# Attention followed by an MoE layer on one core: joined score and value groups on TensorE, and a written order for all engines

## The chip, the core and the metric

The kernel runs on one core of a Trainium2 chip. The metric is the device time of one execution in microseconds. Lower is better. Before the change three runs took 991.96, 991.89 and 991.86 us; the median is 991.89.

The engines in the text: TensorE (PE; its weight loads are PEld), VectorE (DVE), ScalarE (ACT), GpSimd (POOL) and SyncE (SP), which issues most DMAs. Matmul results land in PSUM banks of 512 float32 columns; eight banks exist. All other tiles lie in SBUF.

## The reference

```python
B, H, Sl, Sg, D = 8, 8, 512, 32, 64; window = 32
s_g   = scale * q_g @ [k_g, k_l].T                    # global queries see all keys
out_g = softmax(s_g) @ [v_g, v_l]
s_l   = [scale * q_l @ k_g.T, where(|i - j| <= window, scale * q_l @ k_l.T, -1e9)]
out_l = softmax(s_l) @ [v_g, v_l]                     # local queries: globals and a band
x     = concat([out_g, out_l], tokens) as (B * 544, 512)
h     = x @ w_in                                      # 512 -> 2048
out   = softplus(h) @ w_out                           # 2048 -> 512
```

## The kernel before

A **pair** m is two heads of one batch; there are 32 pairs, four to a batch (m = 4b + j). Pairs 0 to 3 (batch 0) go through an attention of their own at the start (`scores0` to `split0g`). The others run while the second layer already works on an earlier batch.

**The second layer.** A **block** b is one batch: 512 local tokens, 16 **tiles** f of 128 hidden columns. For a tile, `hpart` makes h in one PSUM bank with twelve matmuls of 512 columns (four slices j of x; each the high half xh against both halves of the weights, and the low half xl against one). `act` then makes e: three rows on ScalarE (abs, exp, ln), one on VectorE (line 533, the last reader of the bank of h), gh on ScalarE and gl on GpSimd. `opart` multiplies gh and gl by the output weights into four output banks o0 to o3, six matmuls for two of them. The output half of a tile comes one or two tiles behind its h (`moe_items`). Block 8 is the global tokens of all batches. `split_x` makes xh and xl of the next block from the attention's result xa; slices with odd j on VectorE, the others on ScalarE and GpSimd.

**Attention of a pair.** `scores` makes the scores of 512 queries for two heads in two pieces, p = 0 and 1, with matmuls that use half of TensorE's rows (64x128); each piece fills the two banks of the pool `ps_a`. VectorE adds the mask (line 312) and so copies the piece to SBUF as s; then it takes maxima of 32x32 blocks into mt (313). `maxima` gathers them: GpSimd copies three quarters next to the first (325), VectorE reduces (328 to 332) and copies the result to three more quarters (338). `probs` spreads the maxima as mb (346), GpSimd subtracts (355, 357) and ScalarE takes the exponential (358). `sums` does the same for the sums: zt (368), the gathering, a small addition (371), reciprocals zr (375) and rb (377). `values` makes v_ps with matmuls of half of TensorE's columns (128x64) in the banks of `ps_a`; VectorE multiplies them with rb into xa (396).

**PSUM.** `ps_h` has two banks, which only h uses; `ps_a` has two, for s_ps and v_ps in turn; four are for the output.

**Order.** Behind the start only TensorE's order is written out in full (`mm`); on the other engines the scheduler chooses between what is ready by its own estimate. The attention's steps are a list with a position each (`pieces`): scores of pair m at 12m and 12m + 6, sums at 12m + 14, values at 12m + 21; they are let in between the second layer's items as these advance (48 positions a block). So four pairs pass in a block, each with three separate visits of TensorE: piece 0, piece 1 and the values. Pair 8 begins in block 0.

Of the kernel before, what the change touches and what calls it, by code (L numbers as in the profile page):

```python
# [19 lines left out]
P = 128  # L20
# [3 lines left out]
NPC = 2  # L24
# [9 lines left out]
MPE = 8  # L34
LAG_Z = 6
# [28 lines left out]
def moe_over_global_local_attention(  # L64
# [31 lines left out]
    mask0 = pl.tile([P, 2, 2, 224], BF16, tag="rb", name="mask0", bufs=1)  # L96
# [38 lines left out]
    M = B * H // 2  # L135
    st = {}
# [179 lines left out]

    def grid(t, start, *dims):
        base = t[0:32, start:start + 1]
        return bass.AP(base.tensor, base.offset, [list(base.ap[0])] + [list(d) for d in dims])

    def gather(mt, op):
        for a in range(1, 4):
            nc.gpsimd.tensor_copy(mt[0:32, GW * a:GW * a + GW], mt[32 * a:32 * a + 32, 0:GW])  # L325
        e0 = 4 * GW + 1
        for u, off in ((-1, 2), (2, 3)):
            nc.vector.tensor_reduce(grid(mt, e0 + u, (7, 6), (1, 2)), grid(mt, 4 + u - 2 * (u < 0), (12, 6), (1, 2), (off, 2), (GW, 4)), axis=AX.XY, op=op)
        nc.vector.tensor_reduce(grid(mt, e0 + 1, (7, 6), (4, 2)), grid(mt, 4 + 1, (12, 6), (7, 2), (GW, 4)), axis=AX.X, op=op)
        g = e0 + 42  # L330
        nc.vector.tensor_reduce(grid(mt, g, (1, 2)), grid(mt, 4 + 4, (36, 2), (12, 3), (3, 2), (GW, 4)), axis=AX.XYZ, op=op)
        nc.vector.tensor_copy(grid(mt, e0 + 4, (21, 2), (7, 3)), mt[0:32, g:g + 2].unsqueeze(2).to_broadcast([32, 2, 3]))  # L332
        return mt[:, e0:e0 + 42]

    def maxima(m):
        e = gather(st.pop(("mt", m)), ALU.max)
        for a in range(1, 4):
            i = nc.vector.tensor_copy(e[32 * a:32 * a + 32, 0:40], e[0:32, 0:40]).ins
        order["maxima"] = i
        st["e", m] = e  # L340

    def probs(m, p):
        s, e = st["s", m, p], st["e", m]
        k = QW[p] // 32
        mb = pl.tile([P, 2, 352], F32, tag="mb", name=f"mb{m}_{p}", bufs=2)
        nc.vector.transpose(mb[:, :, :QW[p]].rearrange("p h (s k) -> p h s k", k=32),  # L346
                            windows(e, FIRST[p], 21, 2, k).unsqueeze(3).to_broadcast([P, 2, k, 32]))

        def pairs(t, width, start, step, w):
            base = t[:, 0, start:start + 1]  # L350
            return bass.AP(base.tensor, base.offset, [list(base.ap[0]), [width, 2], [step, 2], [1, w]])

        for so, sd, mo, md, w in (((0, 352, 0, 192, 160),), ((32, 192, 0, 128, 192),))[p]:
            sw = pairs(s, 512, so, sd, w)
            nc.gpsimd.tensor_tensor(sw, sw, pairs(mb, 352, mo, md, w), op=ALU.subtract)  # L355
        for so, mo, w in (((160, 64, 192),), ((0, 64, 32), (416, 224, 96)))[p]:
            nc.gpsimd.tensor_tensor(s[:, :, so:so + w], s[:, :, so:so + w], mb[:, :, mo:mo + w], op=ALU.subtract)  # L357
        nc.scalar.activation(s, s, AF.Exp, scale=0.125)  # L358
# [4 lines left out]

    def sums(m):
        zt = pl.tile([P, rows_of(349)], F32, tag="mt", name=f"zt{m}", bufs=3)
        nc.gpsimd.memset(windows(zt, 0, 36, 3, 4), 0.0)
        for p in range(NPC):
            nc.vector.tensor_reduce(windows(zt, 4 + 16 * p, 36, 2, 16), st["s", m, p].rearrange("p h (b k) -> p h b k", k=32),  # L368
                                    axis=AX.X, op=ALU.add, apply_transpose=True)
        z = gather(zt, ALU.add)  # L370
        nc.vector.tensor_scalar(z[0:32, 0:40], z[0:32, 0:40], 1e-9, None, op0=ALU.add)
        zr = pl.tile([P, ROW], F32, tag="zr", name=f"zr{m}", bufs=2)
        for a in range(4):
            h = a // 2
            nc.vector.reciprocal(zr[32 * a:32 * a + 32, 0:19], z[0:32, 21 * h:21 * h + 19])
        rb = st["rb", m] = pl.tile([P, rows_of(608)], F32, tag="rb", name=f"rb{m}", bufs=1)[:, 0:608]
        nc.vector.transpose(rb.rearrange("p (s k) -> p s k", k=32), zr[:, 0:19].unsqueeze(2).to_broadcast([P, 19, 32]))

    def values(m):
        b, j = divmod(m, H // 2)  # L380
        vt = st.pop(("v", m))
        ps = ps_a.tile([P, 2, 512], F32, tag="a", name=f"v_ps{m}")
        parts = ((0, 0, 0, 160, 0, 0), (1, 0, 160, 192, 0, 64), (2, 0, 352, 160, 0, 192), (2, 1, 0, 32, 0, 352), (3, 1, 32, 96, 0, 288),
                 (3, 1, 128, 96, 1, 0), (4, 1, 224, 192, 1, 32), (5, 1, 416, 96, 1, 128))
        seen = set()
        for c, p, o, w, bank, at in parts:
            for h in range(2):
                mm(ps[64 * h:64 * h + 64, bank, at:at + w], lhsT=vt[:, h, c], rhs=st["s", m, p][:, h, o:o + w],
                   start=(bank, h) not in seen, stop=(c, bank) in ((3, 0), (5, 1)), skip_group_check=True)
                seen.add((bank, h))  # L390
        for p in range(NPC):
            del st["s", m, p]
        rb = st.pop(("rb", m))
        y = xa[b, j] = pl.tile([P, 608], F32, tag="xa", name=f"xa{b}_{j}", bufs=4)
        for bank, at, w in ((0, 0, 384), (1, 384, 224)):
            nc.vector.tensor_tensor(y[:, at:at + w], ps[:, bank, 0:w], rb[:, at:at + w], op=ALU.mult)  # L396
        for o in (352, 576):
            nc.gpsimd.tensor_tensor(y[:, 128:160], y[:, 128:160], y[:, o:o + SG], op=ALU.add)
        nc.sync.dma_start(out=xg_dram[j, :, SG * b:SG * b + SG], in_=y[:, 128:160])
        ready.add((b, j))  # L400

# [3 lines left out]
    def pieces():  # L405
        def piece(*fs):
            def go():
                for f in fs:
                    f()
            return go  # L410
        ps = []
        for m in range(M0, M):
            for p in range(NPC):
                fs = [lambda m=m, p=p: scores(m, p)]
                if m + 1 < M:
                    fs.append(lambda m=m, p=p: load(m + 1, p))
# [4 lines left out]
            ps.append((12 * m + 8 + LAG_Z, lambda m=m: sums(m)))  # L421
            fs = [lambda m=m: values(m)]
            if m + 2 < M:
                fs.append(lambda m=m: load_v(m + 2))
            ps.append((end(m), piece(*fs)))
        ps.sort(key=lambda t: t[0])
        return ps


    def split_x(b, j):  # L430
        xh[j] = pl.tile([P, 512], F32R, tag=f"xh{j}", name=f"xh{b}_{j}", bufs=1)
# [70 lines left out]
    def moe_items():  # L502
# [24 lines left out]
        def act(b, f):  # L527
            ph = g.pop(("ps", b, f))
            e = pl.tile([P, 512], F32, tag="e", name=f"e{b}_{f}", bufs=2)
            nc.scalar.activation(e, ph, AF.Abs)  # L530
            nc.scalar.activation(e, e, AF.Exp, scale=-1.0)  # L531
            nc.scalar.activation(e, e, AF.Ln, bias=one)  # L532
            nc.vector.scalar_tensor_tensor(e, ph, 0.0, e, op0=ALU.max, op1=ALU.add)  # L533
            gh = pl.tile([P, 512], F32R, tag="gh", name=f"gh{b}_{f}", bufs=3)
            gl = pl.tile([P, 512], F32R, tag="gl", name=f"gl{b}_{f}", bufs=3)
            nc.scalar.copy(gh, e)  # L536
            nc.gpsimd.tensor_tensor(gl, e, gh.bitcast(F32), op=ALU.subtract)  # L537
# [14 lines left out]
        def store(b, t):  # L552
            o = pl.tile([P, 512], F32, tag=("gh", "gl")[t % 2], name=f"ot{b}_{t}", bufs=3)
            if b < B:
                if t % 2:
                    nc.scalar.copy(o, po[t])
                else:
                    nc.vector.tensor_copy(o, po[t])
                r = b * S + SG + t * P
                nc.sync.dma_start(out=out[r:r + P, :], in_=o)  # L560
            else:
                nc.scalar.copy(o[:, 0:256], po[t][:, 0:256])
                nc.vector.tensor_copy(o[:, 256:512], po[t][:, 256:512])
# [11 lines left out]
        done = 0  # L575
        for i, (b, f) in enumerate(tiles):
            if f == 0 and b > 0:
                items.append((b, 0, 0, lambda b=b: [split_x(b, j) for j in range(4)]))
# [5 lines left out]
            behind = 1 if (b, f + 1) not in tiles or (f == 0 and b > 0) else 2  # L584
            upto = halves.index(tiles[i - behind] + (0,)) + (2 if tiles[i - behind][0] < B else 1) if i >= behind else 0
            while done < upto:
                second(done, b)
                done += 1
        while done < len(halves):
# [87 lines left out]
    for i, (b, size, w, it) in enumerate(items):  # L677
        it()
# [5 lines left out]
        at = first + 48 * (b + gone[b] / total[b]) if b else START + (first + 48 - START) * gone[b] / total[b]  # L684
        attention(at)
# [59 lines left out]
```

## Time and profile before

| | |
|---|---|
| profiled execution | 991.48 us, of which the span is 989.7 |
| median of three runs | 991.89 us |
| granted TensorE clock, mean | 0.988 |
| TensorE, output matmuls of gh (L132, 1,088) | 344.8 us |
| TensorE, h matmuls of xh (L132, 1,152) | 341.9 us |
| ScalarE rows of e and gh (L530, 531, 532, 536), 136 each | 81.0, 85.9, 98.4, 84.5 us |
| VectorE row of e (L533), 136 | 92.7 us |
| GpSimd row of gl (L537), 136 | 180.5 us |

A row names the line, the engine, the operation and the tiles, then count, busy time and the mean of one. "Idle before" an engine's row is put down to whatever released it last. A chain row gives start, length, engine, tile and line, and how many records it merges; a full matmul is one record, and each float32 matmul of the attention is two. Matmuls of a row overlap, so a group's length is read from start to start.

### The profile page before, as it was taken

What the parts mean: (1) busy time and instruction counts of PE and PEld (TensorE: products, weight loads), DVE (VectorE), ACT (ScalarE), POOL (GpSimd) and SP (SyncE); (2) the same over time, 40 slices, a digit from 0 to 9 for tenths busy, and PEclk for the clock granted to TensorE, in tenths of its full rate; (3) what the DMA queues carried; (4) which work ended last, traced back from release to release, by engine and by line L of the source; (5) the groups of instructions that cost most, each with busy time, mean ns of one, the idle gap of its engine ahead of it and who ended that gap; (6) DMA issues with size and microseconds to landing.
All of it is one profiled execution on the core that took longest, in us unless ns stands there. A gap on an engine that the chain in (4) does not pass through costs nothing.

```text
span 989.7 us, 14732 instructions
## 1 busy us (share of the span) xinstructions
PE 946.2 (96%) x5476; PEld 763.8 (77%) x5476; DVE 643.1 (65%) x1193; ACT 492.6 (50%) x811; POOL 469.5 (47%) x648
## 2 busy tenths in 40 slices
PE   6998598889999999999999999999999999999998
PEld 4776476668888788878887888878887888888896
DVE  5869898896667756786669666776668665411211
ACT  5756466544444544454445444454454445444453
POOL 4437776655445544444445544554445444322221
PEclk8998899999999999999999999999999999999999
DMA  9651331211112211121112111121112100100000
GB/s 357 231 188 46 122 111 57 65 66 41 47 47 69 69 47 46 48 74 47 47 37 72 47 47 47 66 71 47 47 33 88 32 17 1 65 1 1 10 35 22
DMA packets 30697, 64.60 MB, mean 65 GB/s; under 512 B 7328, under 2 KB 7840, under 8 KB 30624
## 3 DMA queue, kind: packets, MB, share of 16 engines
q1 hardware_dynamic: 29888, 63.32, 19.0%
q8 instruction: 43, 0.70, 0.3%
q10 hardware_dynamic: 736, 0.33, 0.2%
q14 instruction: 30, 0.25, 0.1%
HBM read 54.20 MB, written 9.44 MB: 64 GB/s over the span
## 4 chain that ended last, share of the span: by engine, by line
PE 67%; DVE 9%; POOL 4%; issue 3%; ACT 1%; DMA 1%; POOLq 0%; DVEq 0%; ACTq 0%
PE o L132 30%; PE h L132 29%; PE s_ps L132 5%; PE v_ps L132 4%; DVE xh L442 1%; DVE zt L368 1%; DVE xl L443 1%; POOL xl L443 1%; DVE mb L346 1%; POOL mt L325 1%; DVE s L312 1%; POOL s L355 1%; DVE xa L396 1%; DVE mt L332 0%; DVE e L533 0%
## 5 line engine op out<-in xcount | busy, mean ns | idle before, releaser
L132 PE MATMUL h<-xh,wi 128*128 128x512 f32 (+1 forms) x1152 | 341.9, 380 | 6.5 <-DVE e L533 5.8
L132 PE MATMUL o<-wo,gh 128*128 128x512 f32 x1088 | 344.8, 398 | 0.0
L537 POOL TENSOR_TENSOR gl<-e,gh 128x512 fp32r<-128x512 f32 x136 | 180.5, 1327 | 315.7 <-ACT gh L536 263.2
L132 PEld LDWEIGHTS h<-xh,wi 128*128 128x128 f32 x1152 | 211.1, 188 | 51.8 <-DVE e L533 8.9
L132 PEld LDWEIGHTS o<-wo,gh 128*128 128x128 f32 x1088 | 198.8, 188 | 46.0 <-issue 3.3
L533 DVE SCALAR_TENSOR_TENSOR e<-h,e 128x512 f32<-128x512 f32 x136 | 92.7, 682 | 210.1 <-ACT e L532 192.5
L132 PE MATMUL h<-xl,wi 128*128 128x512 f32 (+1 forms) x576 | 217.6, 378 | 0.9 <-DVE xl L443 0.9
L132 PE MATMUL o<-wo,gl 128*128 128x512 f32 x544 | 213.1, 392 | 0.2
L530 ACT ACTIVATE e<-h 128x512 f32<-128x512 f32 x136 | 81.0, 595 | 175.5 <-PE h L132 173.5
L536 ACT CAST gh<-e 128x512 fp32r<-128x512 f32 x136 | 84.5, 622 | 154.7 <-DVE e L533 154.5
L132 PEld LDWEIGHTS h<-xl,wi 128*128 128x128 f32 x576 | 108.4, 188 | 21.7 <-DVE xl L443 1.3
L355 POOL TENSOR_TENSOR s<-s,mb 128x640 f32<-128x640 f32 (+1 forms) x56 | 96.6, 1725 | 57.8 <-DVE mb L346 57.8
L132 PEld LDWEIGHTS o<-wo,gl 128*128 128x128 f32 x544 | 102.4, 188 | 23.2 <-POOL gl L537 1.1
L368 DVE TRANSPOSE_TENSOR_REDUCE zt<-s 128x32 f32<-128x1024 f32 x56 | 69.4, 1239 | 58.9 <-ACT s L358 58.7
L358 ACT ACTIVATE s<-s 128x1024 f32<-128x1024 f32 x56 | 59.4, 1061 | 83.5 <-POOL s L357 47.7
L532 ACT ACTIVATE e<-e,one 128x512 f32<-128x512 f32 x136 | 98.4, 723 | 4.3
L531 ACT ACTIVATE e<-e 128x512 f32<-128x512 f32 x136 | 85.9, 632 | 3.9
L313 DVE TRANSPOSE_TENSOR_REDUCE mt<-s 128x32 f32<-128x1024 f32 x56 | 68.9, 1231 | 3.7 <-ACT s L310 2.9
L132 PE MATMUL s_ps<-raw 64*128 64x192 f32 (+2 forms) x672 | 64.3, 325 | 0.6 <-issue 0.6
L132 PEld LDWEIGHTS v_ps<-s,v 128*64 128x64 f32 x896 | 49.4, 137 | 19.5 <-ACT s L310 6.5
L132 PE MATMUL v_ps<-s,v 128*64 128x96 f32 (+3 forms) x896 | 56.7, 280 | 7.3 <-ACT s L310 5.2
L132 PEld LDWEIGHTS s_ps<-raw 64*128 64x128 f32 x672 | 53.5, 192 | 11.6 <-issue 10.8
(147 smaller groups left out, 886.0 us busy)
## 6 DMA issues: line engine op xcount, KB each, us to landing
raw<-in_qk SPq DMA_DIRECT2D x32, 352.0 KB, 3.0
v<-in_v SPq DMA_DIRECT2D x28, 384.0 KB, 3.0
raw<-in_qk SPq DMA_DIRECT2D x28, 368.0 KB, 3.6
wiraw<-in_w_in SPq DMA_DIRECT2D x16, 512.0 KB, 8.5
woraw<-in_w_out SPq DMA_DIRECT2D x16, 512.0 KB, 7.4
out<-ot SPq DMA_DIRECT2D x32, 256.0 KB, 2.1
v<-in_v SPq DMA_DIRECT2D x4, 512.0 KB, 8.6
raw<-in_qk SPq DMA_DIRECT2D x4, 416.0 KB, 8.3
```

What stands on the lines that cost most here:

```text
L132: order["pe"] = after(nc.tensor.matmul(*a, **k), "pe").ins
L313: order["scores"] = nc.vector.tensor_reduce(windows(mt, 4 + 16 * p, 36, 2, 16), s.rearrange("p h (b k) -> p h b k", k=32), axis=AX.X, op=A ...
L355: nc.gpsimd.tensor_tensor(sw, sw, pairs(mb, 352, mo, md, w), op=ALU.subtract)
L358: nc.scalar.activation(s, s, AF.Exp, scale=0.125)
L368: nc.vector.tensor_reduce(windows(zt, 4 + 16 * p, 36, 2, 16), st["s", m, p].rearrange("p h (b k) -> p h b k", k=32), axis=AX.X, op=ALU.add ...
L443: (nc.vector if j % 2 else nc.gpsimd).tensor_tensor(lo, f(t), hi.bitcast(F32), op=ALU.subtract)
L530: nc.scalar.activation(e, ph, AF.Abs)
L531: nc.scalar.activation(e, e, AF.Exp, scale=-1.0)
L532: nc.scalar.activation(e, e, AF.Ln, bias=one)
L533: nc.vector.scalar_tensor_tensor(e, ph, 0.0, e, op0=ALU.max, op1=ALU.add)
L536: nc.scalar.copy(gh, e)
L537: nc.gpsimd.tensor_tensor(gl, e, gh.bitcast(F32), op=ALU.subtract)
```

## The change

**Joined scores.** For pairs 8 to 31 `scores_all` makes both pieces in one stretch of matmuls. Piece 0 goes to the two banks of `ps_a`, piece 1 to the two banks of `ps_h`, one for each head. The mask of piece 0 is added by one VectorE row, that of piece 1 by two.

**Joined values.** `values_two` makes the values of an odd pair in `ps_a` and of the even pair before it in the two banks of `ps_h`, in one stretch.

**Places.** `later` names the tile of a block at which each step is written: scores at tiles 2, 4, 9 and 11, values of two pairs at 8 and 15, and the other steps in between. Around a group, output halves are put off so that six output matmuls stand right behind it. Pair 8 no longer begins in block 0. At tile 15 the next block's first two slices of x are split ahead of the values.

**Order.** In blocks 1 to 6 every instruction of VectorE, ScalarE and GpSimd runs in the order in which it is written (`inorder`); semaphores still decide when.

**Small rows.** The copies of lines 332 and 338 become `tensor_reduce` over an axis of one. In blocks 2 to 7 the xh casts are all on ScalarE, and xl of slices 2 and 3 is on VectorE. rb has two buffers.

```diff
+MLAST = 7
+S_AT = (2, 4, 9, 11)
+V_AT = (8, 15)
+PRE = (3, 3)
+    def inorder(i):
+        if strict:
+            k = "in " + str(i.ins.engine)
+            order[k] = after(i, k).ins
+        return i
+    def scores_all(m):
+        ps = ps_a.tile([P, 2, 512], F32, tag="a", name=f"s_ps{m}_0")
+        banks2 = [[ps[:, h] for h in range(2)], [ps_h.tile([P, 512], F32, tag="h", name=f"s_ps{m}_1{h}") for h in range(2)]]
+        for p in range(NPC):
+            for c, qs, o, w in PARTS[p]:
...
+        inorder(nc.vector.tensor_tensor(st["s", m, 0], ps, mask[:, 0].unsqueeze(1).to_broadcast([P, 2, 512]), op=ALU.add))
+        for h in range(2):
+            inorder(nc.vector.tensor_tensor(st["s", m, 1][:, h], banks2[1][h], mask[:, 1], op=ALU.add))
...
-            i = nc.vector.tensor_copy(e[32 * a:32 * a + 32, 0:40], e[0:32, 0:40]).ins
+            i = inorder(nc.vector.tensor_reduce(e[32 * a:32 * a + 32, 0:40], e[0:32, 0:40].unsqueeze(2), axis=AX.X, op=ALU.max)).ins
...
+    def values_two(m):
+        values(m + 1, a_banks(m + 1))
+        values(m, [ps_h.tile([P, 512], F32, tag="h", name=f"v_ps{m}_{i}") for i in range(2)])
+        values_out(m)
+        values_out(m + 1)
+    def later():
+        for m in range(MLAST + 1, M):
+            b, i = divmod(m - 4, H // 2)
+            at = NF * b + S_AT[i]
+            put(at, "group", lambda m=m: scores_all(m), lambda m=m: spread(st["mt", m]))
...
+            put(at + 1, "act", lambda m=m: maxima(m, True), *[lambda m=m, p=p: lift(m, p) for p in range(NPC)], lambda m=m: probs(m, 0, False))
+            put(at + 2, "act", lambda m=m: exps(m, 0), lambda m=m: probs(m, 1, False))
+            put(at + 3, "act", lambda m=m: exps(m, 1))
+            if m % 2:
+                at = NF * b + V_AT[i // 2]
+                put(at - 1, "end", lambda m=m: sums_first(m))
+                if i // 2:
+                    put(at, "act", lambda b=b: split_x(b + 1, 0), lambda b=b: split_x(b + 1, 1))
+                put(at, "act", lambda m=m: sums_rest(m))
+                put(at, "group", lambda m=m: values_two(m - 1))
+            else:
+                put(at + 4, "act", lambda m=m: sums_first(m))
+                put(at + 5, "act", lambda m=m: sums_rest(m))
...
-            (nc.vector.tensor_copy if j % 2 else nc.scalar.copy)(hi, f(t))
-            (nc.vector if j % 2 else nc.gpsimd).tensor_tensor(lo, f(t), hi.bitcast(F32), op=ALU.subtract)
+            onv = j >= 2 if 1 < b < B else j % 2
+            inorder((nc.vector.tensor_copy if onv and not 1 < b < B else nc.scalar.copy)(hi, f(t)))
+            inorder((nc.vector if onv else nc.gpsimd).tensor_tensor(lo, f(t), hi.bitcast(F32), op=ALU.subtract))
```

Three places show what moves. The first is on TensorE in block 2, at the second piece of a pair's scores (s_ps_1 is piece 1 before; s_ps_0 is piece 0, and s_ps_10 and s_ps_11 are the two heads of piece 1 in the change). Before:

```order
L132 MATMUL o_1_3031<-wo_825,gh_4_3156 128x512 x2
L132 MATMUL o_1_3031<-wo_825,gl_4_3157 128x512
L132 MATMUL s_ps_1_3268<-raw_1_3047,raw_0_2927 128x32 x2
L132 MATMUL s_ps_1_3268<-raw_1_3047 128x192 x4
L132 MATMUL s_ps_1_3268<-raw_1_3047 128x96 x2
L132 MATMUL o_2_3071<-wo_825,gh_4_3156 128x512 x2
L132 MATMUL o_2_3071<-wo_825,gl_4_3157 128x512
```

And in the change:

```order
L136 MATMUL s_ps_0_3094<-raw_0_3004 128x192 x2
L136 MATMUL s_ps_0_3094<-raw_0_3004 128x160 x2
L136 MATMUL s_ps_10_3095<-raw_1_3006,raw_0_3004 128x32
L136 MATMUL s_ps_11_3096<-raw_1_3006,raw_0_3004 128x32
L136 MATMUL s_ps_10_3095<-raw_1_3006 128x192
L136 MATMUL s_ps_11_3096<-raw_1_3006 128x192
```

The piece stood alone between output matmuls; now it follows piece 0 with nothing in between.

The second place is TensorE behind h of tile 9 of that block, at the scores of the third pair of a block. Before:

```order
L132 MATMUL h_9_3417<-xl_3_2898,wi_935 128x512
L132 MATMUL o_0_3027<-wo_1009,gh_7_3328 128x512 x2
L132 MATMUL o_0_3027<-wo_1009,gl_7_3329 128x512
L132 MATMUL o_1_3031<-wo_1009,gh_7_3328 128x512 x2
L132 MATMUL o_1_3031<-wo_1009,gl_7_3329 128x512
L132 MATMUL o_2_3071<-wo_1009,gh_7_3328 128x512 x2
```

And in the change:

```order
L136 MATMUL h_9_3380<-xl_3_2858,wi_935 128x512
L136 MATMUL o_0_2953<-wo_1126,gh_8_3288 128x512 x2
L136 MATMUL o_0_2953<-wo_1126,gl_8_3289 128x512
L136 MATMUL o_1_2957<-wo_1126,gh_8_3288 128x512 x2
L136 MATMUL o_1_2957<-wo_1126,gl_8_3289 128x512
L136 MATMUL s_ps_0_3408<-raw_0_3123 128x160 x2
L136 MATMUL s_ps_0_3408<-raw_0_3123 128x192 x2
```

Six output matmuls, now of tile 8 instead of tile 7, stand between h and the group, whose second piece goes to the banks of h.

The third place is VectorE at tile 8, ahead of the values' products (zt and zr are a pair's sums, rb their spread reciprocals, xa the product with v_ps, e the row that last reads h). Before, one pair's products:

```order
L533 SCALAR_TENSOR_TENSOR e_7_3323<-h_7_3310,e_7_3323 128x512
L396 TENSOR_TENSOR xa_1_3355<-v_ps_3338,rb_3211 128x384
L396 TENSOR_TENSOR xa_1_3355<-v_ps_3338,rb_3211 128x224
L368 TENSOR_REDUCE zt_3424<-s_0_3175 128x2x16
L368 TENSOR_REDUCE zt_3424<-s_1_3277 128x2x16
L312 TENSOR_TENSOR s_0_3406<-s_ps_0_3397,mask 128x1024
```

And in the change:

```order
L371 TENSOR_REDUCE zt_3263<-zt_3263 32x6
L430 TENSOR_SCALAR zt_3263<-zt_3263 32x40
L434 RECIPROCAL zr_3298<-zt_3263 32x19 x4
L436 STREAM_TRANSPOSE rb_3303<-zr_3298 128x608
L458 TENSOR_TENSOR xa_0_3358<-v_ps_0_3340,rb_3248 128x384
L458 TENSOR_TENSOR xa_0_3358<-v_ps_1_3341,rb_3248 128x224
L458 TENSOR_TENSOR xa_1_3364<-v_ps_3323,rb_3303 128x384
L458 TENSOR_TENSOR xa_1_3364<-v_ps_3323,rb_3303 128x224
L636 SCALAR_TENSOR_TENSOR e_9_3393<-h_9_3380,e_9_3393 128x512
L347 TENSOR_TENSOR s_0_3427<-s_ps_0_3408,mask 128x1024
```

The products of two pairs stand together, right behind the second pair's sums and ahead of the next e row and the next mask row.

More of the change, by code (lines that the diff above doesn't have):

```diff
@@ L420, in pieces, with put @@
                 ps.append((12 * m + 6 * p, piece(*fs)))
[L421 to L425, printed above, removed]
+            if m <= MLAST:
+                ps.append((12 * m + 8 + LAG_Z, lambda m=m: sums(m)))
+                ps.append((end(m), piece(lambda m=m: values(m, a_banks(m)), lambda m=m: values_out(m), lambda m=m: load_v(m + 2))))
         ps.sort(key=lambda t: t[0])
         return ps
+    def later():
+        plan = {}
+        def put(f, what, *fs):
+            plan.setdefault((f // NF, f % NF, what), []).extend(fs)
+        for m in range(MLAST + 1, M):
+            b, i = divmod(m - 4, H // 2)
+            at = NF * b + S_AT[i]
+            put(at, "group", lambda m=m: scores_all(m), lambda m=m: spread(st["mt", m]))
+            if m + 1 < M:
+                put(at, "group", *[lambda m=m, p=p: load(m + 1, p) for p in range(NPC)])
+            put(at + 1, "act", lambda m=m: maxima(m, True), *[lambda m=m, p=p: lift(m, p) for p in range(NPC)], lambda m=m: probs(m, 0, False))
[11 more added lines that the diff above has]
+                put(at + 5, "act", lambda m=m: sums_rest(m))
+        return plan
+    halved = set()
     def split_x(b, j):
+        halved.add((b, j))
         xh[j] = pl.tile([P, 512], F32R, tag=f"xh{j}", name=f"xh{b}_{j}", bufs=1)
@@ L572, in second, with run @@
             items.append((at, 2, 0, lambda: [opart(c, f, t) for t in (t0, t0 + 1)]))
-        done = 0
+        done, plan = 0, later()
+        def run(fs):
+            return lambda: [f() for f in fs]
         for i, (b, f) in enumerate(tiles):
             if f == 0 and b > 0:
-                items.append((b, 0, 0, lambda b=b: [split_x(b, j) for j in range(4)]))
+                items.append((b, 0, 0, lambda b=b: [split_x(b, j) for j in range(4) if (b, j) not in halved]))
                 second(done, b)
@@ L583, in moe_items @@
             items.append((b, 2, w and w + 4, lambda b=b, f=f: (hpart(b, f, (2, 3)), act(b, f))))
-            behind = 1 if (b, f + 1) not in tiles or (f == 0 and b > 0) else 2
+            if (b, f, "act") in plan:
+                items.append((b, 0, 0, run(plan.pop((b, f, "act")))))
+            behind = 1 if ((b, f + 1) not in tiles and (b, f, 'group') not in plan) or (f == 0 and b > 0 and (b, 2, 'group') not in plan) else 2
             upto = halves.index(tiles[i - behind] + (0,)) + (2 if tiles[i - behind][0] < B else 1) if i >= behind else 0
@@ L588, in moe_items @@
                 done += 1
+            if (b, f, "group") in plan:
+                ahead = PRE[f in V_AT]
+                for k in range(ahead - 2):
+                    second(done, b)
+                    done += 1
+                items.append((b, 0, 0, run(plan.pop((b, f, "group")))))
+                second(done, b)
+                done += 1
+            if (b, f, "end") in plan:
+                items.append((b, 0, 0, run(plan.pop((b, f, "end")))))
+        assert not plan, plan
         while done < len(halves):
```

138 lines of the change are left out of this document (90 added, 48 removed).

## The prediction, made before the change was run

> **What bounds the kernel now.** I read the page first, then the busy time by stage, the waits of TensorE, the chain of waits in one block, and one token tile across the engines.
>
> ```profile
> span 989.7 us, 14732 instructions
> PE 946.2 (96%) x5476; PEld 763.8 (77%) x5476; DVE 643.1 (65%) x1193; ACT 492.6 (50%) x811; POOL 469.5 (47%) x648
> ```
>
> TensorE is busy for 96% of the span, the next engine, VectorE, for 65%. By stage (columns: the stretch, its length, busy time and instructions of PE, PEld, DVE, ACT, POOL, then the granted clock, DMA share and GB/s):
>
> ```profile
> 200.00:216.16 16.16, 13.52 (x64) 9.94 (x63) 15.62 (x25) 5.08 (x8) 9.94 (x16) 1.00 0.17 59
> 323.98:431.80 107.82, 107.25 (x624) 86.42 (x624) 75.29 (x143) 51.56 (x79) 52.86 (x80) 1.00 0.17 53
> ```
>
> From 216 us on, a block (one batch) takes 107.82 us, and TensorE works in 107.25 of them at the full clock. Cheaper instructions on VectorE, ScalarE or GpSimd are worth nothing there by themselves: time goes only if TensorE's own row gets shorter, or its few waits. Just before 216 us VectorE is the fuller engine, 15.62 of 16.16.
>
> ```profile
> PE h L132 <- DVE e L533: 4.5, 6, 1.7
> PE v_ps L132 <- DVE s L312: 2.1, 1, 2.1
> ```
>
> The first row, from TensorE's waits between 216 and 980 us, is all that it waits there: 4.5 us in 6 places, where a block starts and h of its third tile needs the bank that the e row of the first one still reads. The second, from the whole run's waits, is one wait at 195 us, in block 0.
>
> **The groups on TensorE.** The chain of waits in a steady block (start, us, engine, tile, matmul records):
>
> ```profile
> 327.00 1.36 PE o L132 x6
> 328.36 1.27 PE s_ps L132 x16
> 329.62 1.58 PE o L132 x6
> 331.21 2.72 PE h L132 x12
> 333.93 1.36 PE o L132 x6
> 335.29 1.96 PE v_ps L132 x32
> 337.24 1.59 PE o L132 x6
> 338.83 2.72 PE h L132 x12
> 341.56 1.36 PE o L132 x6
> 342.92 1.07 PE s_ps L132 x12
> 343.98 1.59 PE o L132 x6
> ```
>
> Twelve full matmuls of 512 columns take 2.72 us, 0.443 ns a column. Six take 1.36, but 1.58 or 1.59 behind each attention group: the exit alone costs 0.23. The first piece of scores (160 + 192 + 160 columns, two halves, two records a matmul) streams 2,048 columns, 0.907 us. It takes 1.07 + 0.23 = 1.30: extra 0.39. Values (32 records, 4,096 columns, 1.813 us) take 1.96 + 0.23 = 2.19: extra 0.38. The second piece takes 1.27 + 0.22 = 1.49: extra 0.58, of which I put the 0.19 beyond the others down to its 32-column part. So the extra belongs to the **group**: 0.38 us for 12 records and for 32.
>
> For pairs 8 to 31 the change makes one group of a pair's two pieces, and one of the values of two pairs. It removes 24 and 12 groups, 36 x 0.38 = **-13.7 us**; the matmuls stay. Bounds: 36 x 0.23 = -8.3, if only the exit that is seen goes; -13.7 - 24 x 0.19 = -18.3, if the small part is hidden too.
>
> **Old waits.** At a block's start the new order puts half an output tile, 1.36 us, between h of tile 1 and h of tile 2. The steady wait there was 0.57 (107.82 less 107.25). I let all **-4.5** go (bounds 0 and -4.5). Pair 8's scores and half of pair 9's leave block 0, and with them the bank that the values waited for at 195 us: **-2.0**. Bounds 0 and -5: the stretch to 216.16 has 16.16 - 13.52 = 2.6 of idle TensorE time more, some of which may go too, since the work that leaves also frees VectorE.
>
> **New waits.** The joined groups take both banks of h, so h and attention now wait for one another. One tile of h across the engines:
>
> ```profile
> 347.91 0.39 PE L132 MATMUL h<-xl,wi 128*128 128x512 f32 x1
> 348.39 0.60 ACT L530 ACTIVATE e<-h 128x512 f32<-128x512 f32 x1 [1.88 <-PE h L132]
> 349.69 0.72 ACT L532 ACTIVATE e<-e,one 128x512 f32<-128x512 f32 x1
> 350.45 0.69 DVE L533 SCALAR_TENSOR_TENSOR e<-h,e 128x512 f32<-128x512 f32 x1 [0.30 <-ACT e L532]
> 351.87 1.29 POOL L537 TENSOR_TENSOR gl<-e,gh 128x512 fp32r<-128x512 f32 x1 [2.40 <-ACT gh L536]
> ```
>
> TensorE goes on to the next group 0.23 after 347.91; the bank has been read at 351.14, **3.0 us later**.
>
> At tile 9 only six output matmuls (1.36) and the first piece (1.07) stand between h and the second piece, which writes that bank: 2.4 us against 3.0. TensorE waits 0.6 once a block, with the restart 0.65: six times, **+3.9**. Bounds: 0, and 6 x 1.4 = 8.4 if one more ScalarE row of 0.72 gets in between. At tiles 2, 4 and 11 eighteen output matmuls stand there, 4.08 + 1.07 = 5.1 us; gh, the tile before and the lifted maxima stand ahead in the queues, and following them I find 0.7 us or more to spare.
>
> Behind a group come six output matmuls, 1.59, then h, which needs the group's first bank of h back.
>
> ```profile
> L312 DVE TENSOR_TENSOR s<-s_ps,mask 128x1024 f32<-128x1024 f32 x48 | 58.2, 1213 | 5.4 <-PE s_ps L132 5.4
> L396 DVE TENSOR_TENSOR xa<-v_ps,rb 128x384 f32<-128x384 f32 x28 | 15.2, 544 | 2.0 <-PE v_ps L132 0.5
> ```
>
> From the group's start the first piece takes 1.07, its mask row 1.21, half of the second's about 0.65 (half a row): 3.1 with the hand-overs. h comes at 1.07 + 1.1 + 1.59 = 3.7. So 0.6 to spare, at no cost while VectorE is free.
>
> The tight place is tile 8, where h of tile 9 needs a bank that the values fill. VectorE's work in the same block by tile, first on mt (four pairs), then on zt:
>
> ```profile
> 323.98:431.80 107.82, 22.97 (x48) 3.59 (x16) 1.00 0.17 53
> 323.98:431.80 107.82, 19.12 (x49) 3.33 (x16) 1.00 0.17 53
> ```
>
> ```profile
> L377 DVE STREAM_TRANSPOSE rb<-zr 128x608 f32<-128x608 f32 x28 | 22.7, 809 | 0.7
> ```
>
> From the odd pair's scores until that h, VectorE has their mask rows (2.5), one pair's mt (22.97 / 4 = 5.7), two pairs' zt (9.6), four e rows (2.8), two rb (0.81 each) and one product (0.54): 22.7 us. TensorE spends 28.3 there: four h and three output tiles at 2.72, three half tiles at 1.36, the second piece and the joined values. In between, e rows stand in the queue before their h is through; following them I count some 4.7 us of that. About 0.5 is left. I take 0.3 a block, and 0.2 at each of six block starts, where the last xl rows end close to their use: **+3.0**. Bounds: 0, and 17 from the L371 row below.
>
> **Edits that cost nothing.** The small copies that become reductions, the mask rows in halves (0.65 each against 1.21 for both: 24 x 0.1 on VectorE) and the xh casts that move to ScalarE (50% busy) lie beside TensorE's row; without that cover they would cost a few us in all. The loads on SP's queue are still asked for a pair ahead, at least five groups of 2.72 us, and land in 3 to 4:
>
> ```profile
> raw<-in_qk SPq DMA_DIRECT2D x28, 368.0 KB, 3.6
> ```
>
> The small rows on VectorE:
>
> ```profile
> L338 DVE COPY mt<-mt x84: 175/177/1176, 68.8 to 819.5; 32x40 f32<-32x40 f32 x84
> L371 DVE TENSOR_SCALAR zt<-zt x28: 168/175/1300, 90.4 to 830.7; 32x40 f32<-32x40 f32 x28
> ```
>
> (min, median, max in ns.) Both mostly take 0.18 us, yet up to 1.18 and 1.30. The Trainium skill (SBUF — State Buffer, "Who interferes with whom") says that a copy or a tensor_scalar can take a port pair that VectorE shares with GpSimd, and then one waits for the other's whole instruction, while a tensor_reduce never contends. The outliers agree with it. By that rule the copies lose their outliers, and the tensor_scalar, which the change leaves as it is, keeps them.
>
> **The sum**, against the profiled execution's 991.48: 991.5 - 13.7 - 4.5 - 2.0 + 3.9 + 3.0 = 978.2. The median of the runs shown is 0.4 higher: **978.6 us**.
>
> **Rivals.**
> *The small row collides (8%).* L371 stands ahead of rb and the products. If both of a double pair were at 1.30 instead of 0.17, tile 8 would lose 2.3 less the 0.5 to spare, and a block start 1.1: 6 x 2.9 = 17 in place of the 3.0, **993**. Against it: a median of 175. At half that rate it is 985. This is what the Trainium skill's rule on the shared pair would give where GpSimd is always reading.
> *The extra belongs to the records (6%).* Then joining groups saves nothing and 978.6 + 13.7 = **992**. Against it: 0.38 for 12 and for 32 records, and the slow six matmuls behind each group. The Trainium skill (TensorEngine Tiling (Array Packing), "Instruction Overhead") puts about 60 cycles on each matmul, which points this way; its "Key Properties" say that a change of tiling mode drains the engine, which points to the group. The rows here side with the second.
> *Slower: the written order holds h's activations back (10%).*
>
> ```profile
> ACT s L358 <- POOL s L357: 47.7, 29, 6.9
> ```
>
> ScalarE waited 47.7 us for GpSimd's subtractions, 1.6 a time. The change writes each exponential at a fixed place ahead of a later tile's first activation. If one in each pair holds an h for 1.6 that has 0.7 to spare, TensorE loses 0.9, 24 times: 21.6, **1000**. It decides from the gain on: 13.3 / 24 = 0.55, so from a hold of 0.55 + 0.7 = 1.25. For it: no bank is left over, and by the queues I followed the exponentials do hold the activations of tiles 6 to 8 for 1 to 2 us. Against it: behind just those tiles 2 us or more remain until their bank is asked for, and GpSimd is busy for 52.86 of 107.82.
> *That the change doesn't do what it says* is ruled out by the order: the groups are joined.
>
> **How the numbers follow.** Forecast 76%, its own range 964 to 985: all gains at their far ends without new waits give 991.9 - 18.3 - 4.5 - 5 = 964; the small exit alone gives 978.6 + 5.4 = 984. The range that should hold the time 8 in 10 is 964 to 990; the slower case and most of the two at 992 lie outside. About 0.2%, 2 us, is what a measurement of this kernel can tell from no change. Faster: 76 + 6 of the collisions = 82%. Same: 2 + 5 = 7%. Slower: 10 + 1 = 11%.
>
> **What would show it.** In the profile after: s_ps in groups of 28 records and v_ps of 64, six output matmuls of 1.59 behind each, blocks near 105.5 us; PE s_ps waiting for e some 0.6 us once a block; h waiting for xa or xl well under a microsecond; no wait of v_ps for s in block 0. Wrong would be: h waiting for s (the mask rows come late), e rows behind exponentials on ScalarE, or output matmuls that are as slow in sum as before.

## The result, and the profile after

The median of four runs is 973.34 us (972.56 to 974.40) against 991.88 us (989.99 to 991.96) for the kernel before on the same chip: a ratio of 0.9818, with a 95% interval of 0.9801 to 0.9835. That is 1.8% faster, 5.3 us less than forecast and inside the range. The profiled execution took 974.09 us.

The page of the kernel after, span and busy time of the engines:

```profile
span 971.8 us, 14734 instructions
PE 933.1 (96%) x5476; PEld 768.9 (79%) x5476; DVE 608.5 (63%) x1193; ACT 497.0 (51%) x835; POOL 467.0 (48%) x648
```

The number of matmul records is the same, and TensorE is busy for 13.1 us less: its row got shorter without losing a matmul. One steady block by stage, from the values at tile 8 of block 3 to those of block 4:

```profile
463.56:568.82 105.26, 104.93 (x625) 87.07 (x624) 69.75 (x143) 52.27 (x82) 52.43 (x81) 1.00 0.18 55
```

A block took 107.82 and now takes 105.26, near the 105.5 that was forecast (the forecast's own terms give 106.1, see below). TensorE's waits from 210 to 960 us (total, times, longest):

```profile
PE s_ps L136 <- DVE e L636: 2.0, 6, 0.3
PE h L136 <- DVE xa L458: 0.8, 1, 0.8
```

The six waits of h for e at block starts are gone. A new one stands six times in their place, of s_ps for e, and one of h for xa in block 2. The chain of waits shows the joined values and the joined scores:

```profile
299.62 3.76 PE v_ps L136 x64
303.38 2.99 PE o L136 x12
306.37 5.44 PE h L136 x24
311.81 1.36 PE o L136 x6
313.17 2.72 PE h L136 x12
315.89 4.08 PE o L136 x18
319.97 2.14 PE s_ps L136 x28
322.10 1.58 PE o L136 x6
```

Groups of 28 and 64 records, and matmuls that are 0.22 to 0.27 late behind each. The two pieces of scores took 1.30 + 1.49 = 2.79 us apart; joined they take 2.14 + 0.22 = 2.36. Two pairs' values took 2 x 2.19 = 4.38; joined, 3.76 + 0.27 = 4.03.

The chain at tile 9 of block 3 has the new wait:

```profile
468.99 2.76 PE h L136 x12
...
473.12 0.73 ACT e L635
...
473.88 0.70 DVE e L636
474.58 0.04 issue
474.62 1.33 PE s_ps L136 x11
475.95 1.59 PE o L136 x6
```

The chain leaves TensorE behind h, goes through the rows that make e, and comes back at the second piece of scores, whose bank e has just finished reading. The wait that the trace names is 0.33 us. What it costs is read from start to start: h ends at 471.75 and the next output matmuls begin at 475.95, 4.20 us, where six output matmuls and a group take 1.36 + 2.14 = 3.50. So it costs 0.7.

The small rows on VectorE (min/median/max in ns):

```profile
L379 DVE TENSOR_REDUCE mt<-mt x84: 184/188/191, 69.0 to 813.6; 32x40 f32<-32x40 f32 x84
L371 DVE TENSOR_REDUCE zt<-zt x28: 145/152/158, 89.0 to 828.6; 32x6 f32<-32x6 f32 x28
L430 DVE TENSOR_SCALAR zt<-zt x28: 167/631/1296, 90.0 to 828.8; 32x40 f32<-32x40 f32 x28
```

The rows that became reductions have no outliers left. The one that stayed a tensor_scalar had a median of 175 before and has 631 now.

### The profile page after: what moved, and what is told of

Read it like the earlier page. It is cut to its first block, busy times and chain, and to the rows that moved or that the text cites. A ratio compares the mean times of both kernels' runs of the same rounds, so it can differ in the third digit from the quotient of the medians.

```text
span 971.8 us, 14734 instructions
## 1 busy us (share of the span) xinstructions
PE 933.1 (96%) x5476; PEld 768.9 (79%) x5476; DVE 608.5 (63%) x1193; ACT 497.0 (51%) x835; POOL 467.0 (48%) x648
## 4 chain that ended last, share of the span: by engine, by line
PE 78%; DVE 3%; ACT 2%; issue 1%; POOL 1%; ACTq 0%; DVEq 0%
PE o L136 34%; PE h L136 34%; PE v_ps L136 5%; PE s_ps L136 5%; DVE e L636 1%; ACT e L635 1%; ACT e L634 0%; ACT e L633 0%; DVE zt L419 0%; DVE zr L434 0%; DVE zt L430 0%; DVE woraw L585 0%; POOL s L401 0%; ACT s L409 0%; POOL s L403 0%
## 5 line engine op out<-in xcount | busy, mean ns | idle before, releaser
L136 PEld LDWEIGHTS o<-wo,gh 128*128 128x128 f32 x1088 | 201.0, 188 | 43.8 <-issue 0.3
L409 ACT ACTIVATE s<-s 128x1024 f32<-128x1024 f32 x56 | 59.3, 1059 | 24.2 <-POOL s L403 24.2
L419 DVE TRANSPOSE_TENSOR_REDUCE zt<-s 128x32 f32<-128x1024 f32 x56 | 66.1, 1213 | 5.0 <-ACT s L409 5.0
L351 DVE TRANSPOSE_TENSOR_REDUCE mt<-s 128x32 f32<-128x1024 f32 x48 | 56.7, 1219 | 0.0
```

Source lines behind the costliest of these rows:

```text
L136: order["pe"] = after(nc.tensor.matmul(*a, **k), "pe").ins
L351: order["scores"] = inorder(nc.vector.tensor_reduce(windows(mt, 4 + 16 * p, 36, 2, 16), st["s", m, p].rearrange("p h (b k) -> p h b k", k=32),
L409: inorder(nc.scalar.activation(s, s, AF.Exp, scale=0.125))
L419: inorder(nc.vector.tensor_reduce(windows(zt, 4 + 16 * p, 36, 2, 16), st["s", m, p].rearrange("p h (b k) -> p h b k", k=32), axis=AX.X, op ...
```

## Experiments

All but one are edits of the kernel after; "+9.6 us" and the like are differences of two ratios times 990 us, uncertain by about 2 us; smaller differences are read from the traces. A block is measured from the values at tile 8 of block 3 to those of block 4.

| kernel | median us | ratio to before (95%) | a block, us |
|---|---|---|---|
| before | 990 to 992 | 1 | 107.82 |
| after | 973.34 | 0.9818 (0.9801 to 0.9835) | 105.26 |
| scores apart | 982.38 | 0.9915 (0.9900 to 0.9929) | 106.65 |
| values apart | 976.94 | 0.9866 (0.9851 to 0.9881) | 106.02 |
| start as before | 973.79 | 0.9831 (0.9816 to 0.9846) | 105.27 |
| no addition | 971.29 | 0.9803 (0.9787 to 0.9820) | 105.27 |
| order free | 1074.17 | 1.0831 (1.0815 to 1.0848) | 121.9 |
| copies back | 996.57 | 1.0054 (1.0038 to 1.0070) | 108.67 |
| one copy back (zt) | 980.68 | 0.9902 (0.9888 to 0.9915) | 106.68 |
| before, with reductions | 985.98 | 0.9949 (0.9936 to 0.9963) | 107.36 |
| one half first | 984.35 | 0.9931 (0.9914 to 0.9947) | 107.22 |
| tile 9 later | 973.59 | 0.9822 (0.9808 to 0.9837) | 105.35 |
| tile 9 later, gl last, no addition | 970.16 | 0.9795 (0.9781 to 0.9808) | 105.03 |
| values sooner, no addition | 967.54 | 0.9770 (0.9757 to 0.9784) | 104.54 |

**Scores apart.** `piece` makes the matmuls of one piece, and `scores_all` keeps piece 1 and the mask rows; piece 0 is put ahead of the output half that stood ahead of the group.

```diff
+    def scores_first(m):
+        ps = st["ps", m] = ps_a.tile([P, 2, 512], F32, tag="a", name=f"s_ps{m}_0")
+        piece(m, 0, [ps[:, h] for h in range(2)])
...
+            put(at, "pre", lambda m=m: scores_first(m))
...
+                if (b, f, "pre") in plan:
+                    items.insert(len(items) - 1, (b, 0, 0, run(plan.pop((b, f, "pre")))))
```

> The pieces of a pair's scores stand apart again, with six output matmuls between them, 24 times; everything else stays (written order, reductions, joined values). Theory (the gain is the group's extra): a joined group and the extra of the six matmuls behind it take 2.36 us, the two apart 2.79, so +0.43 a pair, 4 pairs a block, less some 0.25 of the wait at tile 9, which shrinks since the first piece now stands ahead of the output matmuls: +1.5 a block, +8 to +10 us in all, 981 to 984. Rival (the extra belongs to the records, the gain comes from the written order or the reductions): -1.5 to +1 us, 972 to 975.

It took 982.38 us, +9.6. The chain of waits at one pair:

```profile
319.77 1.07 PE s_ps L136 x12
320.84 1.59 PE o L136 x6
322.43 1.27 PE s_ps L136 x16
323.70 1.59 PE o L136 x6
```

With the six matmuls behind each piece these are 5.52 us, where the joined form takes 1.36 + 2.14 + 1.58 = 5.08: 0.44 a pair. A block is 1.39 longer: 4 x 0.44 = 1.76, less some 0.4 of tile 9's wait. The records are the same, so the extra that a join saves belongs to the visit and not to the records.

**Values apart.** The same, with the odd pair's values ahead of the output half.

```diff
-        values(m + 1, a_banks(m + 1))
...
+                put(at, "pre", lambda m=m: values(m, a_banks(m)))
                 put(at, "group", lambda m=m: values_two(m - 1))
```

> The values of the two pairs stand apart, with six output matmuls between them, 12 times; the scores stay joined. Theory (the group's extra): 4.02 us joined against 2 x 2.19 apart, +0.36, 12 times: +4.3 us, 976 to 979. Rival (records, or written order): 0 within 1 us, 972 to 975.

+4.8 us, and 0.76 a block, 0.38 for each joined group, as expected.

**Start as before.** The half output tile at a block's start goes back ahead of h of tile 1.

```diff
-            behind = 1 if ((b, f + 1) not in tiles and (b, f, 'group') not in plan) or (f == 0 and b > 0 and (b, 2, 'group') not in plan) else 2
+            behind = 1 if ((b, f + 1) not in tiles and (b, f, 'group') not in plan) or (f == 0 and b > 0) else 2
```

> At a block's start the half output tile goes back to where it stood before the change, ahead of h of tile 1, so that h of tile 2 follows h of tile 1 at once. Theory (the old waits at block starts were worth about 0.85 us each with the restart): the wait of h for e comes back at six block starts, +0.85 each, +4 to +6 us, 977 to 980. Rival (the old waits were hidden by something else, which the change left alone): within 1 us of 973.3.

+1.3 us, less than the medians can tell, and 105.27 a block: the rival held. The chain at the start of block 2:

```profile
306.63 2.72 PE h L136 x12
309.35 1.36 PE o L136 x6
310.71 5.44 PE h L136 x24
```

Twenty-four matmuls of h, tiles 1 and 2, run without a gap, though nothing stands between them. So the half output tile is not what removed the old wait. What did is seen on VectorE. Its timeline in the kernel before at the same block start, in front of the e row that h waits for:

```profile
307.94 0.63 DVE L332 COPY mt<-mt 32x6 f32<-32x6 f32 x1
308.61 0.56 DVE L338 COPY mt<-mt 32x40 f32<-32x40 f32 x3
...
312.10 2.53 DVE L442 CAST xh<-xa 128x128 fp32r<-128x128 f32 x2
314.55 2.51 DVE L443 TENSOR_TENSOR xl<-xa,xh 128x128 fp32r<-128x128 f32 x2
...
321.01 1.19 DVE L313 TRANSPOSE_TENSOR_REDUCE mt<-s 128x32 f32<-128x1024 f32 x1
...
323.25 0.67 DVE L533 SCALAR_TENSOR_TENSOR e<-h,e 128x512 f32<-128x512 f32 x1
```

VectorE works without a pause from 307 to 324: casts, halves, a mask row, maxima and sums of a pair stand in line ahead of e, whose activation on ScalarE had ended at 321.4. After the change scores and values stand elsewhere, and the same place reads:

```profile
306.77 0.68 DVE L661 COPY ot<-o 128x512 f32<-128x512 f32 x1
311.24 0.69 DVE L636 SCALAR_TENSOR_TENSOR e<-h,e 128x512 f32<-128x512 f32 x1 [3.78 <-ACT e L635]
```

VectorE stands idle for 3.78 us and waits for ScalarE. The backlog is gone.

**Before, with reductions.** The kernel before, with lines 332 and 338 as reductions and nothing else.

```diff
-        nc.vector.tensor_copy(grid(mt, e0 + 4, (21, 2), (7, 3)), mt[0:32, g:g + 2].unsqueeze(2).to_broadcast([32, 2, 3]))
+        nc.vector.tensor_reduce(grid(mt, e0 + 4, (21, 2), (7, 3)), mt[0:32, g:g + 2].unsqueeze(2).unsqueeze(3).to_broadcast([32, 2, 3, 1]), axis=AX.X, op=op)
...
-            i = nc.vector.tensor_copy(e[32 * a:32 * a + 32, 0:40], e[0:32, 0:40]).ins
+            i = nc.vector.tensor_reduce(e[32 * a:32 * a + 32, 0:40], e[0:32, 0:40].unsqueeze(2), axis=AX.X, op=ALU.max).ins
```

> The kernel before with nothing but the small copies made reductions. Theory (before the change no product was late, and TensorE's waits stood at block starts only, behind VectorE's backlog of casts, sums and maxima): 0 to -2 us, 989 to 991.5; the reductions are worth much only where the joined values make the products urgent. Rival (the reductions are worth the same 23 us in any order): -10 us or more, below 981.

985.98 us, 5.0 less than before: neither 0 to 2 nor 10. A block takes 107.36, 0.46 less, and of the six waits of h for e one is left, in block 1. At the block start above, the row of line 332 now reads:

```profile
304.93 0.15 DVE L332 TENSOR_REDUCE mt<-mt 32x6 f32<-32x6 f32 x1
```

0.15 in place of 0.63: with VectorE's line unbroken up to the e row, the 0.48 comes straight off TensorE's wait. Five blocks give 2.3 us. Another 3.0 lies ahead of the first values of block 1 (224.39 us, before 227.40). There the wait of v_ps for s at 195 us, 2.1 before, is no longer listed.

**Copies back.** The two reductions are copies again; places, order and groups stay.

```diff
-        inorder(nc.vector.tensor_reduce(grid(mt, e0 + 4, (21, 2), (7, 3)), mt[0:32, g:g + 2].unsqueeze(2).unsqueeze(3).to_broadcast([32, 2, 3, 1]), axis=AX.X, op=op))
+        inorder(nc.vector.tensor_copy(grid(mt, e0 + 4, (21, 2), (7, 3)), mt[0:32, g:g + 2].unsqueeze(2).to_broadcast([32, 2, 3])))
...
-            i = inorder(nc.vector.tensor_reduce(e[32 * a:32 * a + 32, 0:40], e[0:32, 0:40].unsqueeze(2), axis=AX.X, op=ALU.max)).ins
+            i = inorder(nc.vector.tensor_copy(e[32 * a:32 * a + 32, 0:40], e[0:32, 0:40])).ins
```

> The two small reductions (one of 6 and three of 40 columns on mt, one of 6 on zt) are copies again, as before the change; all else as after it. Theory (VectorE is beside TensorE's row; a late copy costs only where less than its delay is to spare, at tile 8): 0 to +3 us, 973 to 977, outliers of up to 1.2 us among the copies, and some waits of h for xa. Rival (the reductions make the gain): +10 us or more, above 983.

996.57 us, +23: the rival, and slower than the kernel before. The small row on zt, and TensorE's largest wait over the whole run:

```profile
L371 DVE COPY zt<-zt x28: 153/452/1321, 88.1 to 852.1; 32x6 f32<-32x6 f32 x28
PE h L136 <- DVE xa L458: 15.6, 12, 2.2
```

A row of 0.15 us takes up to 1.32, and h waits for the products xa in twelve places. What holds the row stands beside it on GpSimd; here is the longest, from the timeline:

```profile
356.68 1.31 POOL L640 TENSOR_TENSOR gl<-e,gh 128x512 fp32r<-128x512 f32 x1
356.73 1.32 DVE L371 COPY zt<-zt 32x6 f32<-32x6 f32 x1
```

The copy starts 0.05 behind GpSimd's row and ends 0.06 behind it. So it is each time: 25 of the 28 copies on zt and 25 of the 84 of line 379 took over 0.3 us, and all 50 began while a row of GpSimd ran and ended 0.02 to 0.07 behind it. In the kernel after, 26 of the 28 reductions on zt also began beside a running row of GpSimd, and none took more than 0.16. These are the collisions of the first rival, in the rows that the change had taken out of it.

**One copy back.** Of the rows, only the one of 6 columns on zt.

```diff
+        if op == ALU.add:
+            inorder(nc.vector.tensor_copy(grid(mt, e0 + 4, (21, 2), (7, 3)), mt[0:32, g:g + 2].unsqueeze(2).to_broadcast([32, 2, 3])))
```

> Only the row of 6 columns on zt is a copy again; the rows on mt stay reductions. With all copies back it took 0.65 us in the mean where the reduction takes 0.15, and it stands between the sums and the products that h of tile 9 waits for, twice for a double pair. Theory (the copies cost by this late path: 2 x 0.5 us there, less some 0.6 to spare): waits of h for xa come back and most of the 23 us, +6 to +16 us, 979 to 989. Rival (the copies cost by VectorE's load, of which the three rows of 40 columns a pair have most): 0 to +4 us, 973 to 977.

+8.3 us, in the theory's range, though not most of the 23. `h <- xa` is 6.1 us in six places: 0.96 at tile 8 of most blocks. With all copies back it is 1.8 to 2.2 there, and 0.7 at each tile 15 besides. So the row on zt carries a third of the 23, and the rest needs the rows on mt too. Both theories had a part of it.

**Order free.** In this run `inorder` ties nothing; TensorE's row is unchanged.

```diff
-        if strict:
+        if False:
```

> The written order of VectorE, ScalarE and GpSimd is given up and left to the scheduler; TensorE's order, the joined groups, the places of scores and values and the reductions stay. Theory 1 (the gain is the joined groups and the places on TensorE; the old waits at block starts went because scores and values stand elsewhere, so that VectorE has no backlog there): 0 to +5 us, 973 to 979, and no wait of h for e at block starts. Rival (the written order makes the gain): the waits at block starts come back, or exponentials hold h's activations, +10 us or more, above 983.

1074.17 us, +100: the theory failed by far. TensorE's two largest waits from 200 us on:

```profile
PE o L136 <- POOL gl L640: 37.7, 20, 2.9
PE h L136 <- DVE s L349: 25.3, 18, 3.3
```

The chain of waits at one joined group:

```profile
459.43 1.09 PE s_ps L136 x12
460.55 1.24 DVE s L347
461.81 1.25 DVE mt L351
463.06 1.19 DVE s L349 x2
```

Left free, the scheduler takes the maxima of piece 0 ahead of the mask rows of piece 1, and the banks that h needs come back 1.25 us later. On GpSimd the subtractions go ahead of gl: those of one pair run from 469.22 to 474.39 us, then comes the gl that an output matmul waits 2.88 us for. No wait of h for e at block starts appeared, which agrees that places removed it, not order.

**One half first.** In the second piece the matmuls of one head come first, then those of the other.

```diff
+            turns = [(t, h) for t in PARTS[p] for h in range(2)]
+            if p == 1:
+                turns.sort(key=lambda x: x[1])
+            for (c, qs, o, w), h in turns:
...
```

> In the second piece of a pair's scores the four matmuls of the upper half come first and then the four of the lower, where they took turns; the lower half writes the bank that h's e row still reads at tile 9. Theory (the halves run one behind the other, and only the lower half's bank is late): the wait at tile 9 comes 0.4 us later in the group, so it shrinks from 0.72 to about 0.4 a block: -1 to -2.5 us, 971 to 972.5, and the joined group stays at 2.14 us. Rival (two matmuls on different halves of the array share their time while they take turns): the second piece takes up to twice its 0.9 us, +10 to +20 us.

+11.2 us: the rival. The group in the chain:

```profile
321.59 2.79 PE s_ps L136 x26
```

2.79 in place of 2.14, 0.65 more in each of 24 groups (15.6), while tile 9's wait went (-4.3). The two heads' matmuls, on different halves of the array, share time while they take turns. So the prediction's 0.443 ns a column, taken from full matmuls, fits these only in turns: the second piece's 2,048 columns, 0.907 us by it, take 0.65 more here.

**No addition.** Without line 430.

```diff
-        inorder(nc.vector.tensor_scalar(z[0:32, 0:40], z[0:32, 0:40], 1e-9, None, op0=ALU.add))
```

> Leaves out the addition of 1e-9 to the sums of the exponentials (each sum holds an exponential of nought, so it is 1 or more). It is the one small row on VectorE that the change left as a tensor_scalar; it took up to 1.30 us and made h of tile 9 wait 0.76 us for the product xa in block 2. Theory: that wait goes, -0.8 us, and nothing else: 972 to 973.5. Rival (the row costs more than the wait that is seen, through the queue behind it): -2 us or more, below 971.5.

-1.5 us, within the uncertainty; the median lies below the theory's range and just inside the rival's. Tile 8 of block 2 to that of block 3 takes 105.26 instead of 106.30, and the wait of h for xa is gone: the 0.76 that was seen cost 1.04. The values at tile 8 of block 1 came 1.05 sooner too (250.94 instead of 251.99 us). That lead is there by 200 us, ahead of the steady blocks, and its cause is open. So the theory's wait is shown, with the restart added to its price; "nothing else" is not.

**Tile 9 later.** Twelve output matmuls instead of six ahead of the scores at tile 9.

```diff
-                ahead = PRE[f in V_AT]
+                ahead = 4 if f == 9 else PRE[f in V_AT]
```

> At tile 9 the other half of tile 8's outputs is moved ahead of the scores too, and the first half of tile 9's stands behind them: twelve output matmuls instead of six between h and the scores. Theory (the scores wait there for the bank that e still reads, 0.72 us a block with the restart): the wait goes in all six blocks, -3 to -4.5 us, 969 to 970.5, and the first outputs of tile 9 find gl ready by some 0.5 us. Rival (the 0.72 is not the wait but the group itself, or the outputs of tile 9 come too soon for gl): -1 to +2 us, 972 to 975.

+0.4 us, nothing, as the rival said. The wait of s_ps for e went, and another came, six times again:

```profile
PE o L136 <- POOL gl L640: 3.1, 6, 0.5
```

The outputs of tile 10 now come 1.36 us sooner and find gl not ready. The wait was pushed two tiles on.

**With gl last there, and no addition.** Of the edits, the one at tile 10's outputs:

```diff
+            if f == 10 and t0 == 0 and 0 < c < B - 1:
+                items.append((at, 2, 0, lambda: [opart(c, f, t, k) for k in ((0, 1), (2,)) for t in (t0, t0 + 1)]))
...
```

> The kernel of the run before with twelve output matmuls ahead of the scores at tile 9, and two edits more: the addition of 1e-9 is left out, and in the first half of tile 10's outputs the two matmuls that read gl come last, 0.45 us later each, since they waited 0.51 us for gl there once a block. Theory (the 4.3 us of tile 9's wait turned into that wait for gl): 6 x 0.6 to 0.7 goes, and 1 to 1.5 us of the addition: 967.5 to 969.5, below both kernels. Rival (the time lies in the groups, and no wait that is seen is worth its time): 971 to 973.

970.16 us, -2.3, of which the addition alone gave 1.5: in neither range. A block is 0.24 shorter than without the addition alone; the expectation of 0.6 to 0.7 was not met, though no wait is listed any more. The trace shows the other half: the twelve output matmuls ahead of tile 11's scores take 3.14 us (481.27 to 484.41), where such twelve take 2.81, and that group of scores 2.32 in place of 2.14. These 0.5 us are waits too short for the list.

**Values sooner, no addition.** The output half ahead of the values at tile 8 is taken away, so that it stands behind h of tile 9; line 430 is left out as well.

```diff
-                ahead = PRE[f in V_AT]
+                ahead = 2 if f == 8 else PRE[f in V_AT]
```

> Without the addition of 1e-9 (leaves it out), and the values at tile 8 stand six output matmuls earlier, so that twelve instead of six stand between h of tile 9 and the scores. The wait at tile 9 should go (-0.72 a block); but h of tile 9 then asks 1.36 us sooner for the bank that the product xa reads, with some 0.6 us to spare in four blocks. Theory: h waits for xa by 0.5 to 0.8 us a block instead, -1 to +1 us against the kernel without the addition, 970 to 973. Rival (more is to spare at tile 8 than the 0.6 that is read from the trace): -3 to -4.5 us, 967 to 968.5.

967.54 us, the rival, and the fastest of all: ratio 0.9770, 4.8 us below the change, with intervals that don't meet. The chain at tile 9:

```profile
462.54 1.60 PE o L136 x6
464.14 2.76 PE h L136 x12
466.90 2.72 PE o L136 x12
469.62 2.14 PE s_ps L136 x28
471.75 1.58 PE o L136 x6
```

No gap: a block takes 104.54, 0.73 less than without the addition alone, which is tile 9's whole price. And h does not wait for xa. VectorE there:

```profile
463.32 1.58 DVE L457 TENSOR_TENSOR xa<-v_ps,rb 128x384 f32<-128x384 f32 x4
```

The first of the four products takes 0.52 and ends at 463.84; on the timeline the first matmul of h begins at 463.98, 0.13 later, and it is 0.13 in all six blocks. The expectation had left out that line 430, at 0.35 and 0.66 us in this block of the kernel after, had used up what was to spare: without it 1.49 is to spare (product's end 465.24, h 466.73 in the run without the addition), and 1.36 just fits.

## Why the prediction was right, and where its steps failed

**The groups: right, a little small.** Forecast -13.7. The experiments give 24 x 0.44 + 12 x 0.38 = -15.2. The extra belongs to the group, for 28 records as for 64. The step that was mis-sized is the second piece, whose 0.19 beyond the others was put down to its 32-column part: apart the pieces take 1.07 + 1.27 = 2.34 inside, joined 2.14, with that part still there. That 0.2 went with the group. The Trainium skill (TensorEngine Tiling (Array Packing), "Key Properties") says that a change of tiling mode drains the engine; the runs bear out a price for each change, 0.38 to 0.44 us for leaving and entering once. These visits differ from the matmuls around them in number type too (float32 against fp32r), and no run parts the two. The same page of the Trainium skill puts about 60 cycles on each matmul ("Instruction Overhead"). Were that all of the extra, both joins would have saved nothing; they saved 15.2 us.

**The old waits: right that they go, for a wrong reason.** The prediction said that half an output tile between h of tile 1 and h of tile 2 removes them. Putting it back changed a block by 0.01. That they went all the same is luck, as far as that reason goes. They were VectorE's backlog. The reductions alone take off 0.46 of it a block, and the moved scores and values leave VectorE idle there. The price put on them was too small as well. Before the change the first values of a block came 27.60 us after the ones before them, where the others came 26.74 apart: 0.86, not 0.57, five times, and about 2.0 for the 1.7 at 216 us, so -6.3 for -4.5.

**Tile 9: right.** Forecast +3.9, measured 0.72 a block, +4.3. The three kernels with twelve output matmuls there have no such wait; one of them kept all of the time.

**Tile 8: the slack near, the sum too large.** "About 0.5 is left" does not follow from its own terms, 28.3 - 22.7 - 4.7 = 0.9. Measured in block 3 it is 0.43: the first product ended at 468.40, and the first matmul of h began at 468.83 on the timeline. Of the 3.0 us the trace shows one late place, 1.04 in block 2, which the run without the addition took away. The first rival's row did collide, 27 of 28 times beyond 0.3 us; it used up what was to spare, and made h wait once.

**"Edits that cost nothing": the step that failed.** The reductions were put beside TensorE's row; "without that cover they would cost a few us in all". They carry 23 us in the new order, more than the whole gain. The prediction had the parts: 22.7 of 28.3 us of VectorE's time ahead of tile 8, half a microsecond to spare, copies of up to 1.18 us. It used them for the tensor_scalar alone, and held a median from the old order against that. In the new order the copy on zt has a median of 452 where it had 258, and of the 84 rows of 40 columns on mt 25 are late as copies where one was. The Trainium skill (SBUF — State Buffer, "Who interferes with whom") says that copies and tensor_scalars can contend with GpSimd for a shared port pair and a tensor_reduce cannot. The runs agree on every row: up to 1.32 us as copies, each late one ending with a row of GpSimd, and never above 0.19 as reductions. The other small edits (the xh casts on ScalarE, the mask rows in halves, the second buffer of rb) have no run of their own.

**The written order: its rival was the wrong way round.** The prediction feared that it holds h's activations back, 10% for 1000 us. Without it the kernel takes 1074: the order is what gives the banks of h, and gl, back in time. In the change ScalarE waits 24.2 us for the subtractions where it waited 47.7, and no wait of TensorE's for ScalarE is listed from 210 us on.

**Block 0.** h of tile 2 of block 1 began at 207.74 instead of 216.16. Of the 8.4 us, 4.1 is three pieces of scores that moved to later, 2.0 the wait at 216 us counted above; 2.3 remain, for a forecast of 2.0. No run took this part alone. The reductions made that h 3.0 sooner in the kernel before (213.15), and the wait at 195 us went with them, so they may be the whole of it; that it went because pair 8 left is not shown.

**The sum.** Together: 991.48 - 15.2 - 6.3 - 2.3 + 4.3 + 1.0 = 973.0, against 974.09. About one microsecond is not assigned. For a block: 107.82 - 4 x 0.44 - 2 x 0.38 - 0.86 + 0.72 = 105.16, against 105.26. The "105.5" of the prediction was near, but its terms give 107.82 - 6 x 0.38 - 0.57 + 0.65 + 0.5 = 106.1. The 5.2 us between forecast and sum are mainly three terms off by 1.5 to 2.0 each to the same side (groups, old waits, tile 8).

**Luck.** The prediction would have said nearly the same time for the change without the reductions, and that kernel takes 996.57, above its range to 990. That the change had them, and not the reckoning, kept the forecast right.

## What to carry to other kernels

Where TensorE changes between whole-array and half-array matmuls, count the changes, not the matmuls: each visit cost 0.4 us here, and joining visits pays as long as the banks come back in time. Once groups share banks, the other engines' order has to be written so that the reader of a bank comes first; and a small row on VectorE ahead of it is better of a kind that does not collide with GpSimd, here a reduction in place of a copy. A wait that is moved away tends to come up again a tile or two on, so compare the block's length, not the list of waits.

## What the runs showed of the hardware

A 32x6 copy on VectorE took 0.15 to 1.32 us by what GpSimd did beside it: each of the slow ones began while a row of GpSimd ran and ended 0.02 to 0.07 us behind it. The same row as a reduction took 0.11 to 0.16. Matmuls on the two halves of the array's rows overlapped when they took turns: run one half behind the other, the same 28 records took 2.79 us in place of 2.14. A wait of 0.33 us in the middle of a group cost 0.72 of the block, and one of 0.76 ahead of h cost 1.04.
